# Stage A of batch 0 by halves of d, filters held for x, and V and G loaded within the first stage B

## The chip, the cores and the metric

One core of one Trainium2 chip. The metric is the device time of one execution in microseconds (us). An execution of one kernel repeats to about 0.3%, so every comparison is made between runs of the same rounds on the same chip. A ratio is the mean time of one kernel's fast runs over that of the kernel before in the same rounds, so it is not quite the ratio of the medians that stand beside it.

## The reference

```python
def _attn_ref(x, filt_r, filt_i):                 # x: 8 x 3008 x 256
    X = np.fft.rfft(x, axis=1)
    Y = X * (filt_r + 1j * filt_i)[None, :, :]
    return np.fft.irfft(Y, n=x.shape[1], axis=1).astype(np.float32)

def _moe_ref(x, w_gate, w_val, w_out):            # 24064 x 256, d_ff 1536
    gate = np.maximum(x @ w_gate, 0.0)
    val = x @ w_val
    return (gate * val @ w_out).astype(np.float32)
```

The sequence length is split as 3008 = 94 x 32. Stage A transforms along the 94. Stage B transforms along the 32, multiplies by the filter and transforms back. Stage C (psY) undoes the 94. The result feeds the feed-forward part, block by block of 512 tokens (47 blocks).

## The kernel before

Batch 0 is special, because nothing can be done before it. Its stage A output is turned by VectorE within SBUF; the later batches go through DRAM. These are the parts that the change and the argument touch.

```python
AS = pro.tile([128, NC2, N2 // NC2, D], BF16)     # ONE tile for all of A before the turn

def first_a(i):                                   # stage A, batch 0: 16 of these
    c, j = divmod(i, 4)
    psA = matmul_a(c, j, slice(0, 128))
    nc.scalar.copy(AS[:, 2 * j:2 * j + 2, c, :], psA.rearrange("p (n d) -> p n d", n=2))

def turn_a():
    src = AS.rearrange("p l c d -> p (l c) d").bitcast(FP32).rearrange("p n d -> p d n")
    dst = AT.bitcast(FP32).rearrange("p k d -> p d k")
    for h in range(2):
        cols = slice(h * D // 4, (h + 1) * D // 4)
        nc.vector.transpose(dst[:, cols, :], src[:, cols, :])

def first_b(amid):                                # stage B, batch 0
    cuts = (0, 2, 4, 5, 6)
    for i in range(6):
        fwd(0, i)
        if i > 1:
            inv(0, i - 2, cuts=cuts)              # evicts dsb on ScalarE, stores it to Dbuf (SyncE)
        for e in range(2):
            product(0, i, e, 0)
            product(0, i, e, 1, pool=(i, e) in POOL_U)    # some products on GpSimd
        amid(i)                                   # stage A of batch 1, between
    # ... cut: the last two inverses
```

The order of the start. `hold_gpsimd(t)` is a small copy on GpSimd that reads `t`, so all that GpSimd issues after it waits until `t` has landed. `warm(n)` are n matmuls on junk.

```python
hold_gpsimd(XF[0][:, 4 * q - 8:4 * q])            # first half of x landed
for _ in filters:                                 # then: filter loads, GpSimd's queue
    pass
# ... cut: tables, warm(8), warm(3)
for i in range(16):
    first_a(i)
    # ... cut
place_own()
for a in range(2):
    place_filter(0, a, 0, nc.vector.tensor_copy)  # Ftr copies on VectorE
turn_a()
for i in range(9):
    warm(2)
place_filter(1, 1, 0, nc.scalar.copy)             # Fti copies
place_filter(1, 0, 0, nc.vector.tensor_copy)
# ... cut: second halves of the filters and x of batch 1, by DMA on SyncE

hold_gpsimd(AT[0:32, NG - 1, D - 8:])             # A turned
load_vg(0, DFF // 2)                              # first half of V and G
first_b(amid)
load_d(0, 0, 2)                                   # reload of D: dC <- Dbuf, rows of 512 B
nc.gpsimd.dma_start(..., _ap(Dbuf[0], ...))       # 'last': a 512 B load that waits for D's store
for c in range(2, 4):
    load_vg(c * DFF // 4, (c + 1) * DFF // 4)     # V and G, third and fourth quarter
load_at(1, 0)
for i, f in enumerate(early):                     # the rest of batch 1's stage A
    f()
    if i == 2: load_at(1, 1)
    if i == 4:
        for h in range(2):
            item_c(0, h)                          # psY of block 0: needs dC
# then the 47 feed-forward blocks: psV, psG, prod, psO; stages B of the later
# batches are laid between their steps at fixed places
```

## Time and profile before

| what | kernel before |
|---|---|
| time, median of 3 runs | 900.06 us (899.83 to 901.65) |
| TensorE busy | 97% of the span |
| A turned and ready | 31.5 us |
| last dsb of stage B evicted | 50.25 us |
| store of D; reload of D on the chain of waits | 2.42 us; 7.80 us |
| first psV of the feed-forward part | 65.43 us |

Read it as a race to the last row. After it TensorE is never idle for long, so the whole kernel ends as much earlier as the first feed-forward matmul starts earlier, less whatever is lost on the way. (The chain of waits starts its piece psV at 65.64; the first record of psV is at 65.43. Here "first psV" is the record, in every kernel.) The chain of waits, the windows and GpSimd's timeline of this kernel stand in the prediction below.

### The profile page before, as it was taken

How to read it: one execution, taken by the hardware profiler on the slowest of the kernel's cores; microseconds unless marked ns; L12 is line 12 of the kernel's file. 1: busy time of each engine (PE TensorE's matmuls, PEld its weight loads, DVE VectorE, ACT ScalarE, POOL GpSimd, SP SyncE). 2: the span in 40 equal slices, each digit the busy share in tenths (PEclk: the TensorE clock that was granted, in tenths of full speed). 3: DMA queues.
4: the chain of work that ended last, by engine and by line, in shares of the span. 5: the costliest groups of instructions: out<-in, count | busy, mean ns of one | idle time of the engine just before them, and what ended most of it. 6: DMA issues, size and time to landing. Idle time of an engine off the chain costs nothing.

```text
span 898.4 us, 18964 instructions
## 1 busy us (share of the span) xinstructions
PE 868.5 (97%) x7059; PEld 507.2 (56%) x7180; DVE 573.3 (64%) x870; ACT 501.9 (56%) x892; POOL 365.6 (41%) x361
## 2 busy tenths in 40 slices
PE   8769999999999999999999999999999999999997
PEld 3225555556555665556655666556655566566665
DVE  4817776567665776657766677666766577655553
ACT  5545555555655556555655565655565555555553
POOL 4432499018680386514773166811768000000001
PEclk9879999999999999999999999999999999999999
DMA  9895449443465344553364533763346512231111
GB/s 243 243 214 108 123 127 172 102 117 110 137 155 124 89 138 115 142 138 108 96 162 130 117 102 90 180 139 93 107 139 156 118 31 82 68 87 36 36 30 53
DMA packets 110706, 106.86 MB, mean 119 GB/s; under 512 B 20168, under 2 KB 95464, under 8 KB 109975
## 3 DMA queue, kind: packets, MB, share of 16 engines
q1 hardware_dynamic: 86902, 77.80, 33.7%
q0 software_dynamic: 22992, 26.41, 12.2%
q10 hardware_dynamic: 720, 1.45, 0.5%
q8 instruction: 56, 0.92, 0.4%
q14 instruction: 36, 0.29, 0.1%
HBM read 60.42 MB, written 48.23 MB: 121 GB/s over the span
## 4 chain that ended last, share of the span: by engine, by line
PE 85%; DVE 5%; ACT 4%; DMA 3%; issue 2%; SPq 1%; POOL 1%; DVEq 0%; ACTq 0%
PE psG L488 26%; PE psO L507 25%; PE psV L488 24%; DVE prod L493 3%; ACT vsb L491 3%; PE psF L344 3%; PE psD L415 2%; DMA dC<-Dbuf 2%; PE psA L275 2%; PE psX L385 2%; PE psY L472 2%; SPq L178 1%; DVE AT L291 0%; DMA XF<-in_x_dram 0%; POOL uu L399 0%
## 5 line engine op out<-in xcount | busy, mean ns | idle before, releaser
L493 DVE SCALAR_TENSOR_TENSOR prod<-psG,vsb 128x512 bf16<-128x512 f32 x564 | 389.1, 690 | 265.9 <-ACT vsb L491 255.5
L491 ACT CAST vsb<-psV 128x512 bf16<-128x512 f32 x564 | 332.2, 589 | 263.2 <-PE psV L488 163.5
L488 PE MATMUL psG<-yT,WgT 128*128 128x512 bf16 x1107 | 331.0, 379 | 6.7 <-DVE prod L493 0.5
L507 PE MATMUL psO<-WoT,prod 128*128 128x256 bf16 x2256 | 336.5, 273 | 1.1
L488 PE MATMUL psV<-yT,WvT 128*128 128x512 bf16 x1030 | 315.9, 380 | 0.5 <-ACT asb L351 0.5
L507 PEld LDWEIGHTS <-prod 128*128 128x128 bf16 x2256 | 220.5, 98 | 143.5
L488 PEld LDWEIGHTS <-WgT 128*128 128x128 bf16 x1128 | 110.1, 98 | 136.2 <-issue 3.3
L488 PEld LDWEIGHTS <-WvT 128*128 128x128 bf16 x1128 | 98.8, 98 | 42.3 <-issue 31.1
L260 POOL CAST scr<-prod 128x8 f32<-128x8 bf16 x24 | 4.6, 191 | 260.0 <-DVE prod L493 260.0
L530 POOL DMA_DIRECT2D out_dram<-osb x5 | 2.6, 537 | 196.1 <-ACT osb L520 196.1
L520 ACT COPY osb<-psO 128x512 f32<-128x512 f32 x92 | 53.9, 586 | 27.7 <-PE psO L507 26.3
L401 DVE TENSOR_TENSOR tt<-psX,Ftr 128x512 bf16<-128x512 f32 x96 | 65.2, 682 | 3.0 <-PE psX L385 3.0
L330 POOL TENSOR_TENSOR fold<-XP 128x1024 f32<-128x1024 f32 x24 | 56.5, 2356 | 19.4 <-PE psF L344 19.2
L401 DVE TENSOR_TENSOR uu<-psX,Fti 128x512 bf16<-128x512 f32 x89 | 60.5, 680 | 0.0
L317 POOL DMA_DIRECT2D XP<-in_x_dram x96 | 56.8, 596 | 3.1 <-PE psG L488 1.6
L422 ACT CAST dsb<-psD 128x512 bf16<-128x512 f32 x96 | 51.5, 589 | 11.6 <-PE psD L415 11.4
L331 POOL TENSOR_TENSOR XP<-XP 128x1024 f32<-128x1024 f32 x24 | 56.4, 2351 | 1.9
L472 PE MATMUL psY<-M,dC 96*128 96x94 bf16 (+18 forms) x604 | 38.1, 200 | 8.2 <-DMA dC<-Dbuf 8.1
L477 ACT CAST yT<-psY 128x512 bf16<-128x512 f32 x47 | 27.6, 586 | 30.9 <-PE psY L472 30.6
L351 ACT CAST asb<-psF 128x512 bf16<-128x512 f32 x48 | 25.8, 589 | 30.5 <-PE psF L344 30.5
L351 DVE CAST asb<-psF 128x512 bf16<-128x512 f32 x48 | 30.9, 686 | 18.6 <-PE psF L344 17.0
L479 DVE CAST yT<-psY 128x512 bf16<-128x512 f32 x47 | 32.0, 680 | 15.8 <-PE psY L472 15.8
(74 smaller groups left out, 495.8 us busy)
## 6 DMA issues: line engine op xcount, KB each, us to landing
dC<-Dbuf SPq DMA_DIRECT2D x64, 192.0 KB
XP<-in_x_dram POOLq DMA_DIRECT2D x48, 256.0 KB, 6.0
Dbuf<-dsb SPq DMA_DIRECT2D x23, 512.0 KB
at<-Abuf SPq DMA_DIRECT2D x28, 384.0 KB
XP<-in_x_dram POOLq DMA_DIRECT2D x96, 96.0 KB, 2.7
Abuf<-asb SPq DMA_DIRECT2D x96, 96.0 KB
out_dram<-osb SPq DMA_DIRECT2D x69, 94.0 KB
XF<-in_x_dram SPq DMA_DIRECT2D x15, 256.0 KB
```

The lines of the kernel that those rows point to most:

```text
L317: nc.gpsimd.dma_start(xp[r:r + 24, 0:4:2, :], _ap(x, (b * N1 * N2 + o) * D, [[N2 * D, 24], [47 * N2 * D, 2], [1, 512]]))
L330: tt(t, xp[:, 0:2], xp[:, 2:4], op=ALU.add)
L331: tt(xp[:, 2:4], xp[:, 0:2], xp[:, 2:4], op=ALU.subtract)
L351: copy(asf[:, :, q, :], banks[q])
L401: nc.vector.tensor_tensor(p, psX, filt, op=ALU.mult)
L422: nc.scalar.copy(dsb[:, a, o:o + 2, :], psD[a])
L472: nc.tensor.matmul(psY[:, o:o + w], dCs[b, n2 // 8][:, n2 % 8, h * 128:(h + 1) * 128], M1[:, n1:n1 + w], start=True, stop=True)
L488: nc.tensor.matmul(pt[:, :W], w[:, h, ft * 128:(ft + 1) * 128], yt[:, h, :], start=(h == 0), stop=(h == 1))
L491: nc.scalar.copy(vsb, psV[:, :W])
L493: nc.vector.scalar_tensor_tensor(prod, in0=psG[:, :W], scalar=0.0, in1=vsb, op0=ALU.max, op1=ALU.mult)
L507: nc.tensor.matmul(psO[:, t % 2], prods[ft][:, t * 128:(t + 1) * 128], WoT[:, ft, :], start=(ft == 0), stop=(ft == NFT - 1))
L520: copy(osb[:, t0 % 2:t % 2 + 1], psO[:, t0 % 2:t % 2 + 1])
```

## The change

The intent: let VectorE turn the first half of d while TensorE still works on the second; keep the filters out of x's way; and take the V and G loads out of the stretch in which D is reloaded. With them go three evictions of stage B from ScalarE to VectorE, six more warm matmuls, and one more psA piece ahead of the first psY.

```diff
-    def first_a(i):
-        c, j = divmod(i, 4)
-        psA = matmul_a(c, j, slice(0, 128))
-        nc.scalar.copy(AS[:, 2 * j:2 * j + 2, c, :], psA.rearrange("p (n d) -> p n d", n=2))
+    def first_a(p, s, h):
+        psA = ps.tile([128, 4, D // 2], FP32, tag=fft_tag(True), name="psA")
+        xf = XF[p // 2].rearrange("p (n d) -> p n d", d=D)
+        n = p % 2 * NC2 + 4 * s
+        nc.tensor.matmul(psA, WA[:, 0:128], xf[:, n:n + 4, h * D // 2:(h + 1) * D // 2],
+                         start=True, stop=True)
+        nc.scalar.copy(AS[:, 4 * s:4 * s + 4, p, h * D // 2:(h + 1) * D // 2], psA)
 ... turn_a(h): the same transpose, one half a call
 ... items_a: 3 of batch 1's evictions
+            copy = nc.vector.tensor_copy if (c, j) in ((0, 2), (1, 1), (1, 3)) else nc.scalar.copy
 ... start
-    hold_gpsimd(XF[0][:, 4 * q - 8:4 * q])
+    hold_gpsimd(XF[1][:, 2 * q - 8:2 * q])
+    for s in range(2):
+        for h in range(2):
+            first_a(0, s, h)
+    ... make_back_u
+    for p, h in ((1, 0), (1, 1), (2, 0), (3, 0), (2, 1), (3, 1)):
+        for s in range(2):
+            first_a(p, s, h)
-    for a in range(2):
-        place_filter(0, a, 0, nc.vector.tensor_copy)
-    turn_a()
-    for i in range(9):
+    for h in range(2):
+        turn_a(h)
+    for i in range(12):
         warm(2)
 ... all four Ftr copies now by DMA on SyncE, ahead of batch 1's x
     def amid(i):
+        if i in (2, 4):
+            load_vg((i + 2) // 2 * DFF // 4, (i + 4) // 2 * DFF // 4)
 ... after first_b
-    nc.gpsimd.dma_start(... 'last' ...)
-    for c in range(2, 4):
-        load_vg(c * DFF // 4, (c + 1) * DFF // 4)
-    load_at(1, 0)
     for i, f in enumerate(early):
         f()
-        if i == 2:
-            load_at(1, 1)
-        if i == 4:
+        if i == 5:
             for h in range(2):
                 item_c(0, h)
 ... load_at(1, c) for all c at the first steps of the feed-forward part
```

More of the change, by code (lines that the diff above doesn't have):

```diff
@@ L269, in fft_tag, with turn_a @@
         return turn["tags"][turn["i"] % len(turn["tags"])]
-    def matmul_a(c, j, cols):
-        psA = ps.tile([128, 512], FP32, tag=fft_tag(True), name="psA")
-        o = (c * NC2 % NX2) * D + j * 512
-        nc.tensor.matmul(psA[0:cols.stop - cols.start], WA[:, cols], XF[c * NC2 // NX2][:, o:o + 512],
-                         start=True, stop=True)
-        return psA
-    def first_a(i):
-        c, j = divmod(i, 4)
-        psA = matmul_a(c, j, slice(0, 128))
-        nc.scalar.copy(AS[:, 2 * j:2 * j + 2, c, :], psA.rearrange("p (n d) -> p n d", n=2))
-    def turn_a():
+    def first_a(p, s, h):
[3 more added lines that the diff above has]
+        nc.tensor.matmul(psA, WA[:, 0:128], xf[:, n:n + 4, h * D // 2:(h + 1) * D // 2],
+                         start=True, stop=True)
+        nc.scalar.copy(AS[:, 4 * s:4 * s + 4, p, h * D // 2:(h + 1) * D // 2], psA)
+    def turn_a(h):
         src = AS.rearrange("p l c d -> p (l c) d").bitcast(FP32).rearrange("p n d -> p d n")
         dst = AT.bitcast(FP32).rearrange("p k d -> p d k")
-        for h in range(2):
-            cols = slice(h * D // 4, (h + 1) * D // 4)
-            nc.vector.transpose(dst[:, cols, :], src[:, cols, :])
+        cols = slice(h * D // 4, (h + 1) * D // 4)
+        nc.vector.transpose(dst[:, cols, :], src[:, cols, :])
         ats[0] = AT
@@ L298, in one @@
                 st["asb"] = sb.tile([128, NC2 * D], BF16, tag="asb", bufs=4, name="asb")
-            psA = matmul_a(c, j, slice(128, 128 + NROW))
-            nc.scalar.copy(st["asb"][:NROW, j * 512:(j + 1) * 512], psA[0:NROW])
+            psA = ps.tile([128, 512], FP32, tag=fft_tag(True), name="psA")
+            o = (c * NC2 % NX2) * D + j * 512
+            nc.tensor.matmul(psA[0:NROW], WA[:, 128:], XF[c * NC2 // NX2][:, o:o + 512],
+                             start=True, stop=True)
+            copy = nc.vector.tensor_copy if (c, j) in ((0, 2), (1, 1), (1, 3)) else nc.scalar.copy
+            copy(st["asb"][:NROW, j * 512:(j + 1) * 512], psA[0:NROW])
             if j == 3:
@@ L567 @@
     warm(3)
-    for i in range(16):
-        first_a(i)
-        if i == 3:
-            for n in range(3):
-                make_back_u(n)
+    for s in range(2):
+        for h in range(2):
+            first_a(0, s, h)
+    for i in range(3):
+        make_back_u(i)
+    for p, h in ((1, 0), (1, 1), (2, 0), (3, 0), (2, 1), (3, 1)):
+        for s in range(2):
+            first_a(p, s, h)
     place_own()
-    for a in range(2):
-        place_filter(0, a, 0, nc.vector.tensor_copy)
-    turn_a()
-    for i in range(9):
+    for h in range(2):
+        turn_a(h)
+    for i in range(12):
         warm(2)
@@ L580 @@
     place_filter(1, 0, 0, nc.vector.tensor_copy)
-    for fi, cols in ((0, ((0, 0, 2 * q), (0, 2 * q, 4 * q))), (1, ((1, 0, 4 * q),))):
+    for half in range(2):
         for a in range(2):
-            place_filter(fi, a, 1, nc.sync.dma_start)
-        load_x(1, nc.sync, cols)
+            place_filter(0, a, half, nc.sync.dma_start)
+    load_x(1, nc.sync, ((0, 0, 2 * q), (0, 2 * q, 4 * q)))
+    for a in range(2):
+        place_filter(1, a, 1, nc.sync.dma_start)
+    load_x(1, nc.sync, ((1, 0, 4 * q),))
     nc.sync.dma_start(WF, nc.inline_tensor(fold_h, name="dft_fold").ap())
@@ L600 @@
     load_d(0, 0, 2)
-    nc.gpsimd.dma_start(pro.tile([1, D], BF16, tag="nyq", bufs=2, name="last"),
-                        _ap(Dbuf[0], (N2 * NROW - 1) * D, [[D, 1], [1, D]]))
-    for c in range(2, 4):
-        load_vg(c * DFF // 4, (c + 1) * DFF // 4)
-    load_at(1, 0)
     for i, f in enumerate(early):
         f()
-        if i == 2:
-            load_at(1, 1)
-        if i == 4:
+        if i == 5:
             for h in range(2):
@@ L636 @@
         if b == 1:
-            for c in range(2, 4):
-                at_step(c - 2, lambda c=c: load_at(1, c))
+            for c in range(4):
+                at_step(c, lambda c=c: load_at(1, c))
         else:
```

## The prediction

> **What bounds the kernel now.** I read the page first, then the chain of work that ended last for 0 to 110 us, then the windows of 5 us over the start, then the timelines of each engine and the sizes of the DMA packets there.
>
> ```profile
> PE 868.5 (97%) x7059; PEld 507.2 (56%) x7180; DVE 573.3 (64%) x870; ACT 501.9 (56%) x892; POOL 365.6 (41%) x361
> PE   8769999999999999999999999999999999999997
> PEclk9879999999999999999999999999999999999999
> ```
>
> TensorE is busy 97% of the span; all its idle time lies in the first three slices (22.5 us each). From about 66 us on, the feed-forward blocks keep it full, and the diff touches nothing there. So the change can only move the moment at which the first block starts. The chain shows what that moment hangs on (start, us, what):
>
> ```profile
> 12.01 10.55 PE psA L275 x24
> 22.59 0.59 ACT AS L283
> ...
> 27.27 4.19 DVE AT L291
> 31.50 0.96 DVE Fti L240
> ...
> 49.18 1.07 ACT dsb L422 x2
> 50.28 2.42 DMA Dbuf<-dsb
> 52.85 0.32 SPq L448
> 53.22 7.80 DMA dC<-Dbuf
> 61.06 1.03 PE psY L472 x12
> 62.10 3.54 PE psA L275 x4
> 65.64 0.85 PE psV L488 x2
> ```
>
> Four stretches: stage A ends at 23.2 on TensorE and its evictions; VectorE turns A in two pieces of 4.2 us to 31.5; stage B lasts to 50.25; then come the store of D, its reload (7.8 us), and 4.6 us of TensorE work before the first psV at 65.64. The windows (columns: stretch, length, then busy time and count of PE, PEld, DVE, ACT, POOL; clock; DMA share; GB/s) show the state of the engines:
>
> ```profile
> 25.00:30.00 5.00, 1.38 (x6) 0.47 (x5) 5.00 (x2) 2.75 (x1) 0.00 (x0) 0.99 1.04 338
> 30.00:35.00 5.00, 3.48 (x19) 1.16 (x20) 4.58 (x6) 0.60 (x2) 2.37 (x3) 0.50 0.96 314
> 45.00:50.00 5.00, 5.00 (x43) 1.97 (x42) 1.79 (x4) 4.64 (x9) 0.73 (x1) 1.00 0.61 203
> 55.00:60.00 5.00, 0.00 (x0) 0.00 (x0) 0.00 (x0) 0.00 (x0) 1.76 (x3) 0.72 0.99 178
> 60.00:65.00 5.00, 3.94 (x16) 1.96 (x17) 0.69 (x1) 1.17 (x2) 1.80 (x3) 0.50 1.21 254
> ```
>
> The reader sees two idle stretches of TensorE, each followed by a clock of 0.50: the warm matmuls end at 26.44 and A is ready only at 31.5; and nothing runs from 53.57 to 61.06, while the DMA engines are full. What fills them is on GpSimd's timeline:
>
> ```profile
> 53.86 0.74 POOL L248 DMA_DIRECT2D WvT<-in_moe_w_val_dram  x1
> 54.59 0.73 POOL L248 DMA_DIRECT2D WgT<-in_moe_w_gate_dram  x1
> 55.30 0.74 POOL L248 DMA_DIRECT2D WvT<-in_moe_w_val_dram  x1
> 56.01 0.75 POOL L248 DMA_DIRECT2D WgT<-in_moe_w_gate_dram  x1
> ```
>
> **What the Trainium skill says.** (1) "TensorE: Matmul & The Clock Gate", section What's actually happening: the array falls to half clock after an idle window of about 3.4 us and recovers after a busy one; the window is free-running. The trace agrees: after idle stretches of 5.1 and 7.5 us the clock is 0.50, and comes back only once TensorE has been busy for some us (36.7 and 67.4). (2) "DMA: Bandwidth & Descriptors", section Issuing engines are not separate DMA queues: all queues share the same 16 DMA engines. The trace agrees: with D's reload (SyncE's queue) and the V and G loads (GpSimd's) in flight the DMA share is 0.99 to 1.21, and the reload's 512 B packets fall from about 350 in the microsecond from 55 to about 110 in that from 57, when the 768 B packets of V and G begin. (3) The same page, section Queues, rings and completion order: each DMA engine goes round the queues that have work, packet by packet. That fits this slowing.
>
> **The change part by part.**
>
> *Halves of d.* The intent is plain: the first half's eight copies are the first 12 of 16 evictions, so the first turn could start after the eighth of the last twelve matmuls, at 12.01 + 8 x 0.88 + 0.7 = 19.8 rather than 23.2, and A would be ready at 28.2, 3.3 us earlier. But the built program says otherwise. In the list of VectorE's instructions with their waits, the first turn waits for ScalarE's count to reach 19, and the second turn has no wait at all. ScalarE counts 4 evictions, 3 of I2u, and 12 more: 19. So the first turn waits for all sixteen, as it does in the kernel before (also 19): the halves' strided views of one tile are not told apart. Gain: 0. A is ready at 31.5 again. The two Ftr copies that VectorE loses (0.95 each) had ended at 21.15, before the turn, and gave nothing either.
>
> *Filters held.* Packets of 8 KB tell when x lands: first half 11.9, three quarters about 14.1, all about 16.5. GpSimd issues its filter loads from 14.6 instead of 12.5. The last Fti landed at 25.2; 2.1 us more is 27.3. ScalarE's copy (2.75 us) then ends at 30.0, before its first reader at 33.1. The Ftr copies become four DMAs, the needed two landing by about 26; block 1's x follows by about 29, wanted at 31.9. All in the shadow of the turn: 0.
>
> *Warm matmuls.* 24 instead of 18, at 0.225 us: they end at 22.4 + 5.4 = 27.8, and TensorE's gap shrinks from 5.1 to 3.7 us. A whole free-running window of 3.41 us fits into it seldom (0.3 of 3.4, 8%). So stage B should start at full clock. What is this worth? TensorE does its first fwd and psA pieces (0.64 and 2.02 us) in about 0.4 and 1.0, but then waits for GpSimd's products, which still start at 35.06, after 0.96 of Fti, three products at 0.6 and one ScalarE copy. The first is done at 36.2; the inverse that reads it ran at 36.97 because TensorE was late, and now can at 36.25. That moves ScalarE's evictions and GpSimd's next pair by about 0.5 us. Three evictions (0.58 each) leave ScalarE, busy 4.64 of 5, for VectorE, which has room. Against it, 1.47 us of issues now stand on GpSimd ahead of product (3,1), which ends at about 43.5 instead of 42.97. I take 1.1 us (0.4 to 1.8): the last dsb is evicted at 49.15.
>
> *V and G earlier.* Four loads leave the stretch after 50 and go to about 41 and 45, where the DMA share was 0.51 and 0.61. The last pair still overlaps D's final store a little: 2.42 becomes 2.8, so 51.95. The reload is issued at 52.1. Its first two DMAs, all that the first psY needs, are 768 packets. At the uncontended rate of some 350 to 550 a microsecond (seen at 55 and at 75) they take 2; with 2.1 from issue to first packet and 0.7 to the semaphore, about 4.8: 56.9 instead of 61.06. By then TensorE has done six psA pieces after stage B instead of five.
>
> *After the reload.* At full clock psY takes about 0.55 and one psA 0.88 (instead of two at half clock, 3.54): first psV at 58.4. Before: 65.64, and half clock until 67.45 cost another 0.9, so the equivalent is 66.5. Gain 8.1 us. TensorE's gap is then 47.9 + 5.3 = 53.2 to 56.9, 3.7 to 4.2 us: a whole window fits in 10 to 25% by that reckoning; as little activity may also count as idle, I say 35%. If the clock falls, psY and psA take 1.03 and 1.77 and up to 2 us of the first block run at half: gain about 5.2.
>
> Sum: 0.65 x 8.1 + 0.35 x 5.2 = 7.1; 0.5 off for what collides unseen. 900.06 - 6.6 = 893.5 us.
>
> **The rivals.** (a) The turn does overlap: another 3.3 us, so about 890. For it: the loop's order and the diff's intent. Against: the wait for 19. (b) The reload is slow of itself, since its rows are 512 B and the second pair and block 1's loads stand in the same queue: it stays near 7 us, the clock falls, and only one psA piece and stage B's 1.1 us remain: about 897. For it: 512 B packets still took until 61. Against: the count fell as V and G began. (c) The late filters, or GpSimd's issues between its products, become the bound of stage B: 2 us lost, about 896. For it: DMA shares at or above 1 from 15 to 35. Against: 3 us of slack at ScalarE's copy. (d) The WoT load becomes late, as the first block now ends 7 us sooner: it took 10.4 us, and was wanted 16 us after its issue began; now about 11. A wait of at most 1 us.
>
> **Range and chances.** Clock kept and all hidden: 891.5; clock lost: 894.5; rivals (b) and (c): 896 to 897; (a): 890. So 890.2 to 897 for 8 in 10. A gain of 2% would need 18 us, more than all four stretches can give up here (the idle of TensorE is 12.6 us before 62): chance 0.01. A loss of 2% has no mechanism: 0.01.
>
> **What would show it.** Right: turns at about 23.2 and 27.4 again; A at 31.5; no 0.50 in the clock from 30 to 36; stage B's last dsb near 49; D's reload near 4.8 us on the chain; TensorE's wait for dC near 4 instead of 7.5; first psV near 58.4. Wrong: a first turn that starts near 19.8; a wait of ScalarE or VectorE for Fti after 31; psA waiting for block 1's x; dC still taking 7 us with V and G gone; or the first psO waiting for WoT.

## The result, and the profile after

| | before, same rounds | after |
|---|---|---|
| median (range) | 899.94 us, 4 runs | 898.08 us, 4 runs (895.74 to 898.64) |
| ratio | | 0.9973, 95% from 0.9949 to 0.9997 |
| A ready | 31.5 | 31.84 |
| last dsb evicted | 50.25 | 49.91 |
| store; reload | 2.42; 7.80 | 5.53; 4.6 |
| first psV | 65.43 | 62.79 |

The time fell by about 2 us, a third of the 6.6 predicted, and 898.08 lies above the range on record (890.2 to 897.0). A second comparison of the same two kernels gave less still (run c1 below). First the granted clock on the page of the kernel after:

```profile
PEclk9989999999999999999999999999999999999999
```

The early slice below full clock is still there.

The chain of work that ended last, kernel after (start, us, what):

```profile
27.75 4.06 DVE AT L285
...
49.93 5.53 DMA Dbuf<-dsb
```

The second turn ends as late as before; stage B ends 0.34 us sooner in this run (in the repeat, c1 below, it ends later than before); then the store of D takes 5.53 us where it took 2.42. VectorE's timeline shows both turns as one group and what ended the wait before them:

```profile
23.56 8.25 DVE L285 STREAM_TRANSPOSE AT<-AS 128x2048 f32<-128x2048 f32 x2 [10.21 <-ACT AS L278]
```

The windows of 5 us of the kernel after (columns as in the prediction: stretch, length, then busy time and count of PE, PEld, DVE, ACT, POOL; granted clock; DMA share; GB/s):

```profile
45.00:50.00 5.00, 5.00 (x41) 1.87 (x40) 2.63 (x5) 4.09 (x9) 1.78 (x3) 1.00 1.10 234
50.00:55.00 5.00, 4.08 (x10) 1.30 (x8) 0.00 (x0) 3.31 (x6) 0.00 (x0) 1.00 1.08 329
```

Two things. From 45 to 55 the DMA engines are now full (1.10 and 1.08), where they were at 0.61 from 45 to 50 before: D's store, issued at 49.93, starts into full engines. And the clock still falls after both gaps: its records give 0.50 from 33.01 to 36.43 and from 56.91 to 63.73. GpSimd's timeline says what filled the engines (the second load of each pair, G, follows 0.74 us later):

```profile
41.02 0.75 POOL L248 DMA_DIRECT2D WvT<-in_moe_w_val_dram  x1
...
45.33 0.75 POOL L248 DMA_DIRECT2D WvT<-in_moe_w_val_dram  x1
```

The 768 B packets of these four loads were being moved from 42.6 to 53.7. TensorE's timeline after (start, us, line, operation, then in brackets the idle time before and what ended it):

```profile
22.74 5.34 PE L539 MATMUL psJ<-junk 128*128 128x512 bf16 x24
31.86 0.41 PE L383 MATMUL psX<-AT,F 64*64 64x256 bf16 x8 [3.78 <-DVE AT L285]
...
60.15 1.01 PE L470 MATMUL psY<-M,dC 96*128 96x94 bf16 x12 [6.08 <-DMA dC<-Dbuf]
60.99 2.00 PE L295 MATMUL psA<-XF,WA 128*96 128x512 f32 x2
62.79 1.06 PE L486 MATMUL psV<-yT,WvT 128*128 128x512 bf16 x2
...
146.35 0.19 PE L470 MATMUL psY<-M,dC 96*128 96x64 bf16 x1 [1.75 <-DMA dC<-Dbuf]
```

And the last of these in the kernel before:

```profile
148.12 0.19 PE L472 MATMUL psY<-M,dC 96*128 96x64 bf16 x1 [0.58 <-DMA dC<-Dbuf]
```

The 24 warm matmuls leave a gap of 3.78 us; the wait for dC is 6.08 us, not 4; psY and the psA piece behind it (two records to a piece) run at half clock. Then, at 146 us, in a stretch that the prediction held to be untouched, psY of block 5 waits 1.75 us for batch 1's reload, where it waited 0.58.

To follow the gain through the kernel I use the **lead**: how much sooner the first prod of a feed-forward block starts than in the profiled run of the kernel before (79.14 us for block 1). Of the kernel after it is 2.94 us at block 1, 1.77 at block 5 and 1.86 at block 46.

### The profile page after: what moved, and what is told of

Its sections match the earlier page's. It is cut to its first block, busy times and chain, and to the rows that moved or that the text cites. A ratio compares the mean times of both kernels' runs of the same rounds, so it can differ in the third digit from the quotient of the medians.

```text
span 896.3 us, 19093 instructions
## 1 busy us (share of the span) xinstructions
PE 874.9 (98%) x7186; PEld 507.2 (57%) x7186; DVE 572.8 (64%) x871; ACT 499.9 (56%) x889; POOL 364.6 (41%) x360
## 4 chain that ended last, share of the span: by engine, by line
PE 90%; DMA 5%; DVE 2%; ACT 1%; SPq 1%; issue 1%; POOL 0%; DVEq 0%; POOLq 0%
PE psV L486 27%; PE psG L486 27%; PE psO L505 26%; PE psF L342 3%; PE psD L413 2%; PE psY L470 2%; PE psX L383 2%; DMA dC<-Dbuf 1%; PE psA L295 1%; DMA at<-Abuf 1%; DMA Ftr<-Ftr 1%; DMA Ftr<-in_filt_r_dram 1%; DMA Dbuf<-dsb 1%; DMA XF<-in_x_dram 1%; DVE AT L285 0%
## 5 line engine op out<-in xcount | busy, mean ns | idle before, releaser
L486 PE MATMUL psV<-yT,WvT 128*128 128x512 bf16 x1128 | 336.9, 380 | 0.5 <-ACT asb L349 0.5
L486 PE MATMUL psG<-yT,WgT 128*128 128x512 bf16 x1128 | 335.3, 379 | 0.8 <-ACT dsb L420 0.3
L470 PEld LDWEIGHTS <-dC 96*128 96x128 bf16 x604 | 34.8, 98 | 12.5 <-issue 8.3
```

The lines of the kernel that those rows point to most:

```text
L470: nc.tensor.matmul(psY[:, o:o + w], dCs[b, n2 // 8][:, n2 % 8, h * 128:(h + 1) * 128], M1[:, n1:n1 + w], start=True, stop=True)
L486: nc.tensor.matmul(pt[:, :W], w[:, h, ft * 128:(ft + 1) * 128], yt[:, h, :], start=(h == 0), stop=(h == 1))
```

## The experiments

Three batches, each on one chip with the kernel before beside it: medians of before 899.51, 900.09 and 899.29 us, seven runs each; each kernel ran four times, with correct results. The diffs are against the kernel after, unless it says "on before". Theory S: the V and G loads moved out of the reload now slow the store, so that the move is worth little. The rivals: the held filters do it, or the clock does, or the gain is lost in the steady part.

| run | median us | ratio (95%) | store | reload | first psV | lead at block 1 / 5 / 46 |
|---|---|---|---|---|---|---|
| after | 898.08 | 0.9973 (0.9949 to 0.9997) | 5.53 | 4.6 | 62.79 | 2.94 / 1.77 / 1.86 |
| e1_vg_back | 897.10 | 0.9971 (0.9953 to 0.999) | 2.42 | 5.11 | 61.64 | 3.01 / 2.85 / 2.10 |
| e2_hold_back | 897.86 | 0.9984 (0.9969 to 0.9999) | 5.61 | 3.42 | 62.53 | 3.05 / 2.95 / 3.04 |
| e3_last_vg_after_reload | 895.81 | 0.9963 (0.9948 to 0.9977) | 3.03 | 4.33 | 61.44 | 3.23 / 3.56 / 3.15 |
| e4_two_tiles | 898.00 | 0.9994 (0.9973 to 1.0016) | 4.94 | 3.35 | 59.81 | 5.31 / 4.39 / -1.25 |
| e5_one_more_piece (on before) | 898.56 | 0.9983 (0.9968 to 0.9998) | 2.41 | 7.33 | 64.35 | 1.36 / 2.10 / 1.57 |
| e6_clock_kept | 894.52 | 0.9939 (0.9924 to 0.9954) | 5.91 | 3.14 | 61.01 | 4.77 / 5.51 / 5.00 |
| e7_block1_earlier | 896.82 | 0.9961 (0.9946 to 0.9976) | 5.76 | 3.68 | 62.42 | 2.21 / 3.56 / 3.65 |
| e8_all | 891.85 | 0.9907 (0.989 to 0.9923) | 4.04 | 3.87 | 58.52 | 6.70 / 8.04 / 8.12 |
| c1_after_again | 899.09 | 0.9996 (0.9968 to 1.0024) | 4.97 | 3.46 | 62.46 | 2.72 / 2.61 / 2.44 |
| e10_before_clock (on before) | 897.15 | 0.9971 (0.9951 to 0.999) | 2.42 | 7.31 | 62.33 | 3.42 / 4.16 / 3.36 |
| e11_vg_back_clock | 894.11 | 0.9940 (0.9914 to 0.9965) | 2.43 | 5.10 | 59.77 | 5.98 / 6.72 / 6.57 |
| e9_all_and_clock | 891.72 | 0.9917 (0.9893 to 0.9942) | 4.69 | 3.85 | 57.42 | 8.33 / 9.67 / 8.99 |

(The reload is the piece on the chain of waits; for the kernel after and e9, where the chain goes another way there, it is the time from issue to psY.)

### e1_vg_back: V and G where they were

```diff
-        if i in (2, 4):
-            load_vg((i + 2) // 2 * DFF // 4, (i + 4) // 2 * DFF // 4)
     load_d(0, 0, 2)
+    nc.gpsimd.dma_start(... 'last' ...)
+    for c in range(2, 4):
+        load_vg(c * DFF // 4, (c + 1) * DFF // 4)
```

> The changed kernel with the last two pairs of V and G loads put back after stage B, and the small load from D that held them. Theory (the early V and G packets slow D's store and free its reload): the store falls from 5.5 back to 2.4 to 3.2 us, the reload rises from 4.6 to 7 to 8, the first psV comes at 64 to 65.5 instead of 62.8; time 0.1 to 0.4% below the kernel before, at most 2 us slower than the changed kernel. Rival (the late filters slow the store): the store stays near 5.5 and the time is 2 us or more above the kernel before.

The chain of waits of e1:

```profile
50.88 2.42 DMA Dbuf<-dsb
...
53.76 5.11 DMA dC<-Dbuf
```

With the loads gone from stage B the store takes 2.42 us again, to the hundredth as before: theory S holds for the store. But the reload, with the loads beside it again, took 5.11 us and not the 7 to 8 that it took before. Store and reload together are 7.5 us here and 10.1 in the kernel after, and the total did not change (0.9971 and 0.9973). In the profiled run of e1 something else took the gain: stage B took 19.4 us there and 18.1 in that of the kernel after, because the clock stayed at half for longer (table under e6). The packet records show one reason for the shorter reload: the two DMAs that the first psY needs are 768 packets; in the kernel before 342 to 407 of them had ended when the first V or G packet began (the range covers e5 and e10 too), in e1 and e11 655 to 674. Why V and G's packets come about 0.5 us later in these two is not settled.

### e2_hold_back: the filters held as before

```diff
-    hold_gpsimd(XF[1][:, 2 * q - 8:2 * q])
+    hold_gpsimd(XF[0][:, 4 * q - 8:4 * q])
```

> The changed kernel with only the filters' hold put back to the first half of x. Theory (the hold pushes block 1's x, and with it the first V and G pair, some 3 us later on full DMA engines, so the last pair still moves when D is stored): V and G packets end near 50 instead of 53, the store takes 3 to 4 us instead of 5.5, the first psV near 60.5 to 61.5; time about 0.45% below the kernel before. Rival (the last pair collides with the store wherever the filters stand, since GpSimd issues it at 45 to 47): store 5 us or more, time as the changed kernel, 0.27% below.

The store still took 5.61 us, so the hold is not what slows it. TensorE waited 0.98 us for x at 17.87 and the turn began at 23.91, where the kernel after has 23.56. But seven runs with the later hold and one tile began it between 23.23 and 23.77, and three with the old hold and the old order of stage A between 23.21 and 23.77, so the 0.35 us cannot be told from that spread; neither do the totals tell the two apart.

### e3_last_vg_after_reload: the last pair held until D is back

```diff
-        if i in (2, 4):
+        if i == 2:
     load_d(0, 0, 2)
+    hold_gpsimd(dCs[0, 0][:, 7, D - 8:])
+    load_vg(3 * DFF // 4, DFF)
```

> The changed kernel with the last pair of V and G loads held until D's reload has landed. Theory (that pair made the store 3 us longer): store 2.4 to 3.2 us, reload 4.6, TensorE's gap before psY 3 to 4 us instead of 6.1, first psV near 59 to 60.5; time about 0.6% below the kernel before (894 to 895). Rival (the store is slow for another reason, or the second pair does the same): store above 4.5 us and no gain over the changed kernel.

The chain of waits of e3:

```profile
50.85 3.03 DMA Dbuf<-dsb
...
54.34 4.33 DMA dC<-Dbuf
```

The store costs 3.03 us with one pair in stage B instead of two, and the reload is free of V and G. This is the first version in which the intent of the V and G part comes true: 7.4 us for both, first psV 1.35 us sooner than after. It was expected at 59 to 60.5 and came at 61.44: stage B took 19.2 us in this run, and the clock still fell after the reload (58.18 to 65.01).

### e4_two_tiles: the halves in two tiles

```diff
-    AS = pro.tile([128, NC2, N2 // NC2, D], BF16)
+    AS = [pro.tile([128, NC2, N2 // NC2, D // 2], BF16, name=f"AS{h}") for h in range(2)]
-        nc.scalar.copy(AS[:, 4 * s:4 * s + 4, p, h * D // 2:(h + 1) * D // 2], psA)
+        nc.scalar.copy(AS[h][:, 4 * s:4 * s + 4, p, :], psA)
     # turn_a(h) reads the whole of AS[h]
```

> The changed kernel with A's evictions in two tiles, one for each half of d, so that the first turn waits for 15 of ScalarE's instructions and not for 19. Theory: the first turn starts near 20.2 and A is ready near 28.5 instead of 31.8, but ScalarE's copy of Fti, which waits for filters that land at 28.4, ends at 31.2 and holds the first uu; products start 1 to 2 us earlier, not 3.3; the end gains 0 to 1.5 us over the changed kernel, since the store of D still waits behind V and G. Rival (the turn is all that counts): products at 29.5 instead of 32.8 and 3 us gained.

In the built program the first turn now waits for ScalarE's count to reach 15 and the second for 19. VectorE's and TensorE's timelines of e4:

```profile
20.00 8.33 DVE L285 STREAM_TRANSPOSE AT<-AS 128x2048 f32<-128x2048 f32 x2 [5.85 <-ACT AS L278]
...
30.61 0.69 DVE L399 TENSOR_TENSOR uu<-psX,Fti 128x512 bf16<-128x512 f32 x1 [0.58 <-ACT Fti L240]
```

```profile
30.68 1.07 PE L295 MATMUL psA<-XF,WA 128*96 128x512 f32 x2 [1.89 <-DMA XF<-in_x_dram]
...
185.99 0.64 PE L383 MATMUL psX<-at,F 64*64 64x256 bf16 x6 [2.46 <-DMA at<-Abuf]
```

The turn starts at 20.00 and A is ready at 28.35, 3.5 us sooner: that is what the first part of the change was for. It uncovers two waits that 3 us of slack had hidden: 0.58 us for ScalarE's Fti copy and 1.89 us of TensorE for batch 1's x, whose first load the added Ftr copies push back in SyncE's queue (issued at 23.42, and at 20.90 in the kernel before; that this is the whole cause is not shown, see e8). Store and reload still run beside V and G; the lead at block 1 is 5.31 us. The profiled run then lost all of it: 1.51 us ahead of the psY at 143.7, 2.46 us for `at` at 186, with half clock from 185 to 192 after it. That run took 901.62 us; the other three took 897.37 to 898.18, so they lost less, but they have no trace, and why they did not keep 5 us is open.

### e5_one_more_piece (on before): psY one psA piece later

```diff
-        if i == 4:
+        if i == 5:
             for h in range(2):
                 item_c(0, h)
```

> The kernel before with one thing of the change alone: six psA pieces instead of five stand before the first block's psY, one instead of two after it. Theory (this is where most of what the change keeps comes from: at half clock a psA piece costs 1.8 us between psY and the first psV, while before psY it fills idle time): psY to first psV 2.7 us instead of 4.4, time 1.5 to 2 us below the kernel before. Rival (the gain comes from the early V and G loads): no change beyond 0.5 us.

The store (2.41) and the reload (7.33) are those of before; only the stretch from psY to psV shrinks, from 4.37 to 2.66 us, as one psA piece instead of two stands behind psY at half clock. Ratio 0.9983, lead 1.36 at block 1. The kernel after has 0.9973 and, in its repeat, 0.9996, so a single changed digit gives a good part of what the change gives.

### e6_clock_kept: more warm matmuls in both gaps

```diff
-    for i in range(12):
+    for i in range(18):
         warm(2)
         if i == 5:
+            warm(20)
             for h in range(2):
                 item_c(0, h)
```

> The changed kernel with more matmuls on constant data in TensorE's two gaps: 36 instead of 24 while A is turned, and 20 ahead of the first psY. Theory (the clock falls because the prediction's gap of 3.7 us in the first place and 6.1 in the second leave a window with little work): the clock stays at 1.00 through both, psY takes 0.6 and psA 0.9 instead of 1.0 and 2.0, the first psV comes 1.2 to 1.6 us after psY starts instead of 2.6, time 1.5 to 2.5 us below the changed kernel (0.45% below before). Rival (the clock matters little because the evictions bound that stretch): under 0.7 us.

The clock is 1.00 from 6.8 us to the end. The chain of waits of e6:

```profile
49.98 5.91 DMA Dbuf<-dsb
...
56.35 3.14 DMA dC<-Dbuf
59.63 0.62 PE psY L470 x12
60.25 0.93 PE psA L295 x2
```

After the reload the clock is worth 1.3 us in this run: from the start of psY to the first psV it takes 1.38 us, where the kernel after takes 2.64; and the first block runs at full clock.

In stage B it is worth nothing against the profiled run of the kernel after (A ready to last dsb evicted is 18.1 us in both), but that run was lucky. Set side by side, the traces with one tile for A show what half clock costs there:

| the clock is back, us after A is ready | runs | stage B, us |
|---|---|---|
| it never fell | e6, e11, e10 (on before) | 18.1 |
| 3.7 to 4.6 (half clock for 3.41) | after, e2, e7 | 18.1 |
| 5.3 (half clock for 6.83) | before | 18.8 |
| 6.0 to 6.5 (half clock for 6.83) | c1, e3, e1, e5 (on before) | 19.2 to 19.4 |

The repeat c1 is the same program as the kernel after. So in stage B a kept clock is worth 0 to 1.3 us, by when half clock begins and how long it lasts. The evictions moved to VectorE show no effect: before, e5 and e10 don't have them, and stand where the others stand.

### e7_block1_earlier: stage B of batch 1 three steps sooner

```diff
-            l = -35 + 5 * i if b == 1 else -40 + 6 * i
+            l = -38 + 5 * i if b == 1 else -40 + 6 * i
-        at_step(end - 2, lambda b=b: load_d(b))
+        at_step(end - (5 if b == 1 else 2), lambda b=b: load_d(b))
```

> The changed kernel with stage B of block 1 and the reload of its D three steps of the feed-forward earlier. Theory (part of the gain is given back at about 146 us, where psY waits 1.75 us for that reload against 0.58 in the kernel before): that wait is gone, the lead over the kernel before stays near 2.9 us from the first block to the fifth, time 1 to 1.5 us below the changed kernel. Rival (the lead is lost elsewhere, or block 1's loads are not there yet): a new wait near 78 us for block 1's A, or the same time.

The wait at 146 us is gone, and the lead grows from 2.21 at block 1 to 3.56 at block 5 instead of shrinking. (From block 1 to 3 its lead isn't comparable: e7 does the same stage B work earlier there.) At block 5 it leads the kernel after by 1.8 us and the repeat c1 by 1.0. The 1.2 us that the kernel after gave back were lost in this one wait. Its size differs from run to run (the repeat c1 kept its lead from block 1 to 5), so it is a wait that is just met or just missed.

### e8_all: the repairs together

```diff
 e4 (two tiles) + e3 (last pair after the reload) + e7 (batch 1 three steps sooner)
+            warm(8)                                  # ahead of item_c at i == 5
-            for a in range(2):                       # order of the filter loads
+            for a in (0, 1) if dst is Ftr else (1, 0):
-    load_x(1, nc.sync, ((0, 0, 2 * q), (0, 2 * q, 4 * q)))
+        load_x(1, nc.sync, ((0, 2 * q * half, 2 * q * half + 2 * q),))   # between the halves of Ftr
```

> All together: two tiles so that the turn overlaps, the imaginary filters' second half loaded first so that ScalarE's copy of it is not late, block 1's x ahead of the filters' second halves, the last V and G pair after D's reload, 8 matmuls on constant data ahead of psY, and block 1's stage B three steps earlier. Theory: A at 28.4, no wait for Fti above 0.3, store near 3, reload near 4, first psV near 57.5 to 59; time 5 to 7 us below the kernel before (893 to 894.5). Rival (the gain is given back whatever is done, as in the run with two tiles): 896 or above.

The chain of waits of e8:

```profile
48.15 4.04 DMA Dbuf<-dsb
...
52.65 3.87 DMA dC<-Dbuf
```

891.85 us, ratio 0.9907: better than both kernels, and the lead holds to the end (6.70 at block 1, 8.12 at block 46). A is ready at 28.0. Left over: TensorE still waits 2.0 us for batch 1's x, although half of it now stands ahead of two of the Ftr copies, and 2.6 for dC.

### c1_after_again, e10_before_clock, e11_vg_back_clock, e9_all_and_clock

Four runs on one chip, to see how firm the small ratios are and what the clock is worth without the change.

```diff
 c1: the kernel after, unaltered
 e10 (on before):  9 x warm(2) -> 17 x warm(2);  warm(28) ahead of item_c at i == 4
 e11: e1, with 18 x warm(2) and warm(14) ahead of item_c
 e9:  e8, with warm(20) instead of warm(8)
```

> The changed kernel once more, unaltered, as a control beside the other three on one chip. All theories: ratio 0.997 to 0.998 to the kernel before, two falls of the clock, store near 5.5 us, reload 3.5 to 4.6 us.

Ratio 0.9996, interval 0.9968 to 1.0024, with two of its four runs at 900.25 and 901.93. Its chain of waits:

```profile
49.70 1.07 ACT dsb L420 x2
50.80 4.97 DMA Dbuf<-dsb
```

The store is slow again, the clock falls twice again, and the lead at block 1 is 2.72. One thing differs: the first half clock lasts from 30.85 to 37.68, and stage B 19.2 us instead of 18.1. So the change gains little: 0.03 to 0.3% is what both intervals allow.

> The kernel before with only matmuls on constant data added in its two gaps: 34 instead of 18 while A is turned, and 28 ahead of the first psY. Theory (keeping the clock is worth more than the change's own parts): the clock stays at 1.00, two psA pieces after psY take 1.8 instead of 3.5 us, the first block starts at full clock; 2.5 to 3.5 us below the kernel before, which is more than the changed kernel gains. Rival (the fillers only delay psY, or the reload bounds all): under 1 us.

0.9971: fillers alone, on the kernel before, give about 2.5 us, as much as the whole change. The reload there is 7.31 us, as before; stage B takes 18.1 us instead of 18.8, and psY to psV 2.25 instead of 4.37.

> The changed kernel with the last two V and G pairs back after stage B, and with the clock kept by matmuls on constant data (36 in the first gap, 14 ahead of psY). Theory (the early V and G loads are worth nothing in sum, since the store loses what the reload gains): the same time as the changed kernel with the clock kept, 0.994 of before, within 1 us. Rival (the early loads help, and only the clock hid it): 1.5 us or more slower than that kernel.

0.9940 with V and G after stage B and the clock kept, against 0.9939 for e6, which differs from it by having V and G within stage B. Loading V and G earlier is worth nothing in the totals, with the clock kept (e6 and e11) or lost (after and e1); in the profiled runs the first psV even comes later with it, at 61.01 against 59.77 and at 62.79 against 61.64.

> The fastest version so far with 20 instead of 8 matmuls on constant data ahead of the first psY. Theory: TensorE's gap before psY falls from 2.6 us to under 0.5, the second fall of the clock is gone, psA and the first matmuls of the first block run at full clock: 1 to 1.5 us below that version, about 0.990 of before. Rival (the window falls anyway, or the fillers delay psY): the same time or slower.

891.72 us and 0.9917, against 891.85 and 0.9907 of e8: the same within the intervals. The profiled run of e9 kept the clock throughout, where that of e8 has half clock from 30.24 to 33.65 and from 57.55 to 60.96, and its lead at the end is 0.9 us larger. But it was the fastest of the four (891.30), and the mean clock of the others, 0.995 to 0.997 against 1.000, says that it fell in them.

## Why the prediction was wrong

**The turn: right.** It was to wait for all sixteen evictions, as the wait for 19 in the built program said; it started at 23.56 (23.2 predicted) and ended at 31.81. e4 shows that two tiles are what it takes, and that A is then ready 3.5 us sooner, close to the 3.3 that rival (a) put on it.

**The filters: right for their own readers, but a cost was missed.** Fti's copy ended at 31.23, before its first reader at 33.43. The Ftr copies in SyncE's queue come ahead of batch 1's x; in the kernel after that stays hidden, in e4 TensorE waits 1.89 us for x.

**The warm matmuls: wrong, in how a gap was set against a window.** I gave a loss of the clock 8%, since a gap of 3.7 us seldom holds a whole window of 3.41 us. It fell in all eight profiled runs with 24 warm matmuls. In all fourteen traces every stretch of the clock records, but for the cut ones at the ends, is a whole multiple of 3.41 us (in the kernel after 27.31, 3.41, 20.48 and 6.83), so I laid that grid through each trace and took TensorE's busy share of each window, from its records:

| at | busy share of the window | then |
|---|---|---|
| full clock | 0.43 or less, 29 windows | fell to half, all 29 |
| full clock | 0.44 to 0.49, 5 windows | one fell (0.47), four did not |
| full clock | 0.55 or more | never fell |
| half clock | 0.89 or less, 16 windows | stayed at half, all 16 |
| half clock | 0.92 or more, 21 windows | back to full, all 21 |

Two of these windows, the one before the fall in the kernel after and the first at half clock in c1 (columns as above):

```profile
29.60:33.01 3.41, 1.15 (x10) 0.39 (x10) 3.35 (x3) 1.63 (x1) 1.14 (x2) 1.00 1.06 329
30.85:34.26 3.41, 2.64 (x14) 0.71 (x18) 3.35 (x5) 1.51 (x1) 2.36 (x3) 0.50 1.12 294
```

So a window needn't be idle throughout. A gap of 3.7 us that a boundary cuts in two leaves one window with 46% of work at most (an estimate: 1 - 1.85/3.41), so the loss was close to certain. How long it lasts is luck: the fall at 33.01 came after TensorE was at work again, and the next window was full; in c1 the next window was busy for 0.77 only, and half clock lasted twice as long. Of the 1.1 us that I credited to the clock and to the moved evictions, 0.7 came out in the profiled run (18.8 to 18.1), by that luck and not by the warm matmuls; in c1 stage B took 19.2, more than before.

**The store of D: the step that failed.** The prediction: "The last pair still overlaps D's final store a little: 2.42 becomes 2.8". It became 5.53. I took the DMA share of 45 to 50 from the kernel before (0.61) as room for the loads, but the later pair, issued at 45.33, was still moving when the store began at 49.93, because the first pair and batch 1's traffic were in the engines too (share 1.10). The packets show where the time went. In SyncE's queue an earlier store of D (2048 B packets) and one of A (4096 B) stood ahead; their last packets ended at 48.9 and 50.3 in the kernel before, and at 52.4 and 53.7 in the kernel after. So the packets of D's last two stores (1024 B) moved from 51.7 to 55.1 instead of 50.0 to 52.4: what the loads held up was mostly the queue ahead of the store. The mechanism was in the prediction, even with a name; its size was not: 2.7 us too small, the largest term of the miss. e1 (store 2.42 without these loads) and e3 (3.03 with half of them) show the cause. The Trainium skill's "DMA: Bandwidth & Descriptors", section Issuing engines are not separate DMA queues, says that DMAs of all issuing engines run on the same 16 DMA engines; I had used it for the reload and not for the store.

**The reload: right.** 4.8 predicted, 4.6 measured; rival (b) is refuted: free of V and G the reload took 3.1 to 4.6 us in all runs.

**After the reload: the less likely branch.** The wait for dC was 6.08 us, not 3.7 to 4.2, because of the store; the clock fell, which I had at 35%; psY and psA took 2.64 us instead of 1.5. (By the window table, a wait of 3.7 to 4.2 us would hardly have kept it either; 35% was too low.)

The first psV was due at 58.4 and came at 62.79. The 4.4 us are: 0.8 from a later end of stage B (49.15 to 49.91), 2.7 from the store, -0.2 from the reload and its issue, 1.1 from the half clock. In the repeat c1 it is 4.1, with more in stage B (50.77) and less in the store (4.97) and the reload. (Two ends of the range were also reckoned short: 900.06 - 8.1 is 892.0 and 900.06 - 5.2 is 894.9, where the prediction has 891.5 and 894.5.)

**The steady part: not untouched.** The diff does not touch it, but it moved: 1.2 of the 2.94 us of lead went into the wait at 146 us (e7 removes it; in c1 only 0.1 went). WoT, rival (d), was never waited for.

In sum: of the three ideas, the halves never overlapped (one tile), the V and G loads cost the store at least what they saved the reload, and what the hold saved is within the spread of the runs. What gain there is comes from a side effect, one more psA piece before psY (e5, 1.4 us of lead at block 1); the stage B that was 0.7 us shorter in the profiled run was luck.

**Open.** Why TensorE waits for batch 1's x in e8 as long as in e4; why three runs of e4 kept less than their start promised; why the V and G packets begin later in e1 and e11 than in the kernel before; and how much of 0.3% the change gains.

## What to carry to other kernels

Look up in the built program what a split instruction really waits for: strided halves of one tile were waited for as a whole, and only two tiles made the turn overlap. A load moved out of one wait that hangs on the DMA engines lands in the next: reckon all its packets, until the last has landed, against every transfer on the critical path, not only the one that it leaves. When a start moves earlier, the waits far behind it that were just met move with it, so follow the lead through the kernel; and filler matmuls ahead of the first dense stretch can be the cheapest gain of all. Judge a gap by the share of work that it leaves in a window, not by whether it fills one, and look at a second run before you credit a stretch of full clock to the change.

## What the Trainium skill lacked or had wrong

- "TensorE: Matmul & The Clock Gate", What's actually happening: it gives an idle window of about 3.4 us as what lowers the clock and a busy one as what raises it, and leaves open how idle and how busy. Here a window with 43% of work or less always lowered it, one with 55% or more never; 92% or more always raised it, 89% or less never (table above). So a gap of 3.78 us was enough, and the kernel before stayed at half clock through 6.4 us of work (61.06 to 67.45), since its window from 60.62 was busy for 0.87 only. The page's statement that the window is free-running agrees: the first fall came at 29.9 us in the kernel before, and at 33.01 and 30.85 in two runs of the kernel after.
- The same page, Terms, reckons the penalty of a lowered clock as its time times 1 - K/N (K of N clock pulses pass), which at half clock is half of the time: by that estimate 1.7 us for 3.41 and 3.4 us for 6.83. Stage B lost nothing to the first and 0.7 to 1.3 us to the second (18.1 against 18.8 to 19.4), as other engines set much of its pace: in the kernel after the chain of waits runs over VectorE and ScalarE from 31.84 to 39.27, in c1 over TensorE from 31.62 to 38.04.
- "DMA: Bandwidth & Descriptors", Issuing engines are not separate DMA queues: it says that the DMAs of all issuing engines interleave, and gives no figure for what one loses. Here a store of D took 2.42 us without and 4.94 to 5.91 with two pairs of V and G loads in flight (after, c1, e2, e4, e6, e7), most of the difference spent behind delayed stores of its own queue, and a reload with rows of 512 B 3.1 to 4.6 us without them and 5.1 to 7.8 beside them.
- No page has how strided views of one tile are waited for; this is set when the program is built, not by the chip. The first turn waited for a count of 19 with one tile and 15 with two, and A was ready 3.5 us sooner.
